# Block 1's values loaded as bands, queries in mod-3 order, and a new order of the first two blocks in a chunked-attention and gated feed-forward kernel

## The chip, the cores and the metric

The kernel runs on one core of a Trainium2 chip. The metric is the device time of one execution in microseconds, lower is better. Thirteen runs of the kernel before the change gave a median of 246.38 us (244.04 to 248.43).

## The reference

Attention in chunks of 32 queries, each seeing 16 keys to the left of its chunk, the chunk, 8 keys to the right, and 8 memory keys; then a feed-forward layer with a relu gate on the 3072 tokens of 512 features.

```python
# q, k, v: (4, 8, 768, 64); mem_k, mem_v: (4, 8, 8, 64), float32
chunk, left_ctx, right_ctx = (32, 16, 8)
for c in range(S // chunk):
    k_ctx = k[:, :, max(0, 32*c - 16):min(S, 32*c + 40)]        # v_ctx the same
    scores = 1/sqrt(D) * q_c @ concat([mem_k, k_ctx]).T
    a = softmax(scores)
    out[:, :, 32*c:32*c+32] = a @ concat([mem_v, v_ctx])
x = out.transpose(0, 2, 1, 3).reshape(3072, 512)
y = (relu(x @ w_gate) * (x @ w_val)) @ w_out                    # d_ff = 1536
```

## The kernel before

The tokens are cut into 8 blocks of 384 (half a batch element each), a block into 4 steps of 96 queries (three chunks). A step works on a band of 120 keys plus the 8 memory keys, so a score tile is 128 keys by 8 heads x 96 queries. A mask blanks the keys that a chunk may not see: either as a product on DVE after the exponent (`mask`), or as a matmul of the identity with large negative numbers ahead of the scores (L250).

For each block: `load3` loads k and q so that a partition holds three tokens in a row (768-byte runs), `cast3` casts to fp16, a turn brings features onto partitions, `bands` copies the turned keys into four bands. Queries thus come out of the turn in mod-3 order (all tokens 0, 3, 6..., then 1, 4, 7...). A step is `scores` (S), exponent `soft` (x), values (P), `norm` (n), turn of x (T) and its copy into `xT` (e). A block's feed-forward part is 12 units of `dff` (4 gate matmuls, 4 value matmuls of 384 columns, relu on ACT, product on DVE) and 3 of `outp` (12 matmuls of 512 columns).

Blocks 0 and 1 (`EARLY`) are the head. There TensorE does the turns itself. Keys of block 0 go into bands by products with a selection matrix (`keys`, L368). Values of both blocks are loaded in 768-byte runs, cast, and brought into bands by such products too (`gather_v`, L405, four steps for each block, three matmuls of 512 columns for a step; two of the eight steps take more: 28 in all), then evicted (L540). Queries are put back into natural order when they are evicted (`turn_q3` into `qp`). The memory values come by `vm16` and two transfers to the band tiles. Fillers (`keep`, tokens d2, d3, L424) are matmuls on zeros.

The schedule is manual: each engine runs its instructions in program order. In the head this order is written out in `ORDER`, one token for each piece of work (ck, cq, cv casts; key, q, kt, G products and turns; a suffix :D, :A, :P puts the copy on DVE, ACT, POOL; wa, wb, wc are loads of the feed-forward weights on POOL's queue). After `ORDER` stand 22 units for blocks 0 and 1 with hooks, of which the first ones matter here:

```python
pl(raw["k"][0:1, 0, 0, 0, 0:1], w_gate_sb[0:1, 0, 1023:1024])  # POOL, after wc's gate half has landed
load_kq(2)                                                     # waits for the line above
load_w(1024, 512)
hook = {1: cast k of block 2 on ACT, 2: the rest, turn_k(2), 3, 4: the same for q, then load_v(2, 0..3),
        4: pl(gate, w_val_sb[last column]), load_wo(0),        # POOL, after the last weights have landed
        6: bands(2, pl), 7: pl(gate, vraw...), load_wo(4), load_wo(8), ...}
su, vu = (10, 12, 14, 16), (12, 14, 16, 17)                    # units with scores and values of block 2
```

The remaining blocks run in a loop: during block n's feed-forward units, block n+1's four steps (scores at units 4, 6, 8, 10, values two units later) and block n+2's loads, casts and turns. SP's queue takes all loads but the weights, the turns by transfer, and the stores.

Of the kernel before, what the change touches and what calls it, by code (L numbers as in the profile page):

```python
# [7 lines left out]
F32 = mybir.dt.float32  # L8
# [7 lines left out]
def kernel(  # L16
# [42 lines left out]
    opool = ctx.enter_context(tc.tile_pool(name="opool", bufs=3))  # L59
# [20 lines left out]
    v16 = wpool.tile([128, 2, H, R3, D], F16, name="v16")  # L80
    kn = wpool.tile([128, 2, R3 + 1, HP, 2 * D], F16, name="kn")
    qn = wpool.tile([128, 2, HP, R3, 2 * D], F16, name="qn")
    qp = wpool.tile([128, 2, HP, MB], F16, name="qp")
    kx = wpool.tile([2 * NMEM, 2, H, D], F32, name="kx")
    vx = wpool.tile([NMEM, H, D], F32, name="vx")
    kx16 = wpool.tile([2 * NMEM, H, D], F16, name="kx16")
    vx16 = wpool.tile([NMEM, H, D], F16, name="vx16")
    vm = wpool.tile([NMEM, H, D], F32, name="vm")
    vm16 = wpool.tile([NMEM, NJ, H, VW], F16, name="vm16")
# [23 lines left out]
    neg, masks, nat = {}, {}, {}  # L113
# [18 lines left out]
    def natural_mask(name):  # L132
        nat[name] = wpool.tile([128, QB], F16, name=f"nat_{name}")
        pool.tensor_scalar(out=nat[name], in0=neg[name], scalar1=-1.0, scalar2=None, op0=ALU.is_ge)

    def product_mask(name):
        masks[name] = wpool.tile([128, QB], F16, name=f"mask_{name}")
        pool.tensor_scalar(out=masks[name].rearrange("p (t c) -> p t c", t=R3),
                           in0=neg[name].rearrange("p (c t) -> p t c", t=R3), scalar1=-1.0, scalar2=None,
                           op0=ALU.is_ge)  # L140
# [17 lines left out]
    def load_kx(eng, b):  # L158
        eng.dma_start(kx[0:NMEM, b % 2], rows(k, b, MB, NMEM))
        eng.dma_start(kx[NMEM:2 * NMEM, b % 2], mem_k[b].rearrange("h n d -> n h d"))  # L160

    def load_kq(n):
        load3(sp, "k", n)
        if n % 2 == 0:
            load_kx(sp, n // 2)
        load3(sp, "q", n)
# [31 lines left out]
    def bands(n, eng, part=range(6)):  # L198
# [25 lines left out]
        if 5 in part:  # L224
            if i == 0:
                eng(dst(3, 112, [[1, NMEM]]), src(kT, R3 * TS, [[1, NMEM]]))
            if early:
                eng(dst(0, BAND, [[128, NJ], [1, NMEM]]), src(kb_t[0], BAND, [[0, NJ], [1, NMEM]], NJ * 128))
            else:
                eng(dst(0, BAND, [[128, NJ], [1, NMEM]]), src(kT_t[0], R3 * TS + NMEM, [[0, NJ], [1, NMEM]]))  # L230
# [5 lines left out]
    class Step:  # L236
# [7 lines left out]
        def scores(self):  # L244
            i, j = self.n % 2, self.j
            if self.pm:
                m = neg[self.kd]
                m4 = bass.AP(tensor=m.tensor, offset=m.offset, ap=[m.ap[0], [0, HP], [1, QB]])
                for x in range(2):
                    pe.matmul(PS[:, self.sb + x, 0:HP * QB].rearrange("p (a c) -> p a c", a=HP), lhsT=id16, rhs=m4,  # L250
                              start=True, stop=True)
            for a in range(HP):
                for x in range(2):
                    r = slice(D * x, D * x + D)
                    o = PS[:, self.sb + x, QB * a:QB * a + QB]
                    if self.early:
                        pe.matmul(o, lhsT=self.kb[r, a, j, :], rhs=qp[r, i, a, QB * j:QB * j + QB],  # L257
                                  start=not self.pm, stop=True, skip_group_check=self.pm)
                    else:
                        pe.matmul(o.rearrange("p (t c) -> p t c", t=R3), lhsT=self.kb[r, a, j, :],  # L260
                                  rhs=qT_t[i][r, a, :, PP * j:PP * j + PP], start=True, stop=True)
# [7 lines left out]
        def mask(self):  # L269
            e = self.ex[:, :, 0:QB]  # L270
            m = (nat if self.early else masks)[self.kd]
            m8 = bass.AP(tensor=m.tensor, offset=m.offset, ap=[m.ap[0], [0, H], [1, QB]])
            dve.tensor_tensor(out=e, in0=e, in1=m8, op=ALU.mult)  # L273
# [18 lines left out]
        def turn_pe(self):  # L292
            self.t16 = PS[:, 2, 4 * VW:4 * VW + 192].bitcast(F16).rearrange("p (f c) -> p f c", f=4)
            for f in range(NFC):
                pe.transpose(self.t16[:, f], self.x[:, 128 * f:128 * f + 128], id16[0:QB, 0:QB])  # L295
# [19 lines left out]
    def product(n, m, vl_ps, g_relu):  # L315
        if n not in gvT:
            gvT[n] = gvpool.tile([128, NDC, MB], F16, name="gvT")
        if n in EARLY:
            dve.tensor_tensor(out=gvT[n][:, m], in0=vl_ps, in1=g_relu, op=ALU.mult)  # L319
        else:  # L320
            dve.tensor_tensor(out=gvT[n][:, m].rearrange("p (t j c) -> p t j c", t=R3, j=NJ),  # L321
                              in0=vl_ps.rearrange("p (j t c) -> p t j c", t=R3, j=NJ),
                              in1=g_relu.rearrange("p (j t c) -> p t j c", t=R3, j=NJ), op=ALU.mult)
# [7 lines left out]
    def outp(n, t, last=False):  # L331
        o = bank()
        for m in range(NDC):
            pe.matmul(PS[:, o], lhsT=gvT[n][:, m, 128 * t:128 * t + 128], rhs=w_out_sb[:, m, :],  # L334
                      start=(m == 0), stop=(m == NDC - 1))
        o_sb = opool.tile([128, DM], F32, name="o_sb")
        if n in EARLY:
            dst = out[n * MB + 128 * t:n * MB + 128 * t + 128, :]
        else:
            dst = bass.AP(tensor=out.tensor, offset=out[n * MB + t, 0].offset,  # L340
                          ap=[[R3 * DM, 128], [1, DM]])
# [43 lines left out]
    def turn_q3(n, a0):  # L385
# [4 lines left out]
        return qp[:, n % 2, a0:a0 + 2].rearrange("p a (i t) -> p a i t", t=R3), o.rearrange("p a t i -> p a i t")  # L390

    def cast_v3(eng, n, h0=0, nh=H):
        eng(v16[:, n % 2, h0:h0 + nh], vlong[:, n % 2, h0:h0 + nh])

    def gather_v(n, j):
        i = n % 2
        o = PS[:, bank()].rearrange("p (h d) -> p h d", h=H)
        s0 = DPAD + starts[NJ * i + j]
        mm = [(step3[:, s0 - MB * i - t:s0 - MB * i - t + BAND], v16[:, i, :, t, :]) for t in range(R3)]
        if (i, j) == (0, NJ - 1):  # L400
            mm.append((selx[0:NMEM, 0:BAND], vx16))
        if (i, j) == (1, 0):
            mm += [(step3[:, s0 - t:s0 - t + BAND], v16[:, 0, :, t, :]) for t in range(R3)]
        for e, (w, r) in enumerate(mm):
            pe.matmul(o[0:BAND], lhsT=w, rhs=r, start=(e == 0), stop=(e == len(mm) - 1))  # L405
        return vb_t[i][0:BAND, j, :, 0:D], o[0:BAND]
# [3 lines left out]
    for c in "kqv":  # L410
        load3(sp, c, 0, 0, 4)
        if c == "k":
            load_kx(sp, 0)
        if c == "q":
            sp.dma_start(vm, mem_v[0].rearrange("h n d -> n h d"))
        load3(sp, c, 0, 4, 4)
    sp.dma_start(vx, rows(v, 0, MB, NMEM))
# [10 lines left out]
    dve.memset(warm, 0.0)  # L428
    dve.memset(step3, 0.0)
    dve.memset(selx, 0.0)  # L430
    dve.memset(vm16[:, :, :, D:VW], 1.0)
    act.activation(warm, warm, ACT.Exp)
    steps(step3, -DPAD, -R3)
    steps(selx, -(BAND - NMEM), -1)
# [17 lines left out]
    for n in EARLY:  # L452
# [5 lines left out]
    load3(sp, "k", 1)  # L458
# [3 lines left out]
        kx16:A ck00:D mlast:P key0 ck01:D cq00:P key0e:A key2 key2e:A cq01:D d2 key3 vm16:D key3e:A d3 q01 q01e:A  # L462
        cv00:A d2 key1 q00 ke key1e:D q00e:A cv01:P d3 G2 vx16:P S0 kee:A ck10:P x0:A g2:D ck11:D wa:P G0 g0:A M0:D
        S1 cq10:P G1 G3 x1:A cv10:P P0 g3:A M1 cv11:P S2 g1:D kt1 cq11:D x2:A n0:D q11 d3 P1 q11e:A kt1e:D n1:D M2
        T0 q10 kt0 kt0e:D S3 e0:A q10e:A b0:D P2 T1 x3:A M3 wb:P bm:D G4 e1:A S4 n2:D P3 bi2:D T2 G5 g4:A bi0:D
        x4:A wc:P bi1:D n3:D S5 b3:P S6 g5:D e2:A T3 M4 P4 G6 x5:A S7 e3:D x6:A n4:D g6:A M5 M6:D fg01 P5 T4 n5:D
        x7:A G7 e4:A M7:D fg03 fr01:A g7:A P6 T5 fr03:A fg00 fv03 n6:D fg02 fm03:D e5:A P7 fr00:A T6 n7:D fv00 fv02
        e6:A T7 fv01 fm00:D fr02:A e7:D fg10 fm02:D fg12 fr10:A fg13 fm01:D fr12:A fg11 fr13:A fv13 fv12 fr11:A
        fv11 fm13:D fv10 fm12:D fm11:D fm10:D
    """.split()  # L470
    dve_masks = [int(t[1]) for t in ORDER if t[0] == "M" and t.endswith(":D")]
    for i, s_ in enumerate(st):
        s_.pm = i not in dve_masks
    out_of = {}
    for tok in ORDER:
# [7 lines left out]
        elif nm == "vm16":  # L483
            eng(vm16[:, :, :, 0:D], bass.AP(tensor=vm.tensor, offset=vm.offset,
                                            ap=[vm.ap[0], [0, NJ], [D, H], [1, D]]))
            sp.dma_start(vb_t[0][BAND:128], vm16)
            load3(sp, "q", 1)
            load3(sp, "v", 1)
            sp.dma_start(vb_t[1][BAND:128], vm16)
        elif nm == "vx16":  # L490
            eng(vx16, vx)
        elif nm == "mlast":
            build_mask("last", NQB - 1)
            for m in {st[i].kd: 0 for i in dve_masks}:
                natural_mask(m)
        elif nm[:2] in ("ck", "cq"):
            cast3(eng, nm[1], r[0], 2 * r[1], 2)
        elif nm[:2] == "cv":
            cast_v3(eng, r[0], 4 * r[1], 4)
# [24 lines left out]
        elif c == "w":  # L524
            if nm == "wa":
                pl(gate, raw["k"][0:1, 1, 4, 0, 0:1])
            load_w(*{"a": (0, 256), "b": (256, 256), "c": (512, 512)}[nm[1]])
# [9 lines left out]
        elif c == "G":  # L537
            out_of[nm] = gather_v(r[0] // NJ, r[0] % NJ)
# [16 lines left out]
    for m in ("first", "int", "last"):  # L555
        product_mask(m)
# [70 lines left out]
    for n in range(2, NBLK):  # L627
# [3 lines left out]
        for u in range(NDC + NT):  # L631
# [5 lines left out]
            if u >= NDC:  # L637
                for f in mid:
                    f()
                outp(n, u - NDC, last=(n == NBLK - 1 and u == NDC + NT - 1))  # L640
# [57 lines left out]
```

## Time and profile before

| | |
|---|---|
| median of 13 runs | 246.38 us |
| profiled execution | 244.04 us, span of its instructions 242.3 us |
| granted TensorE clock | 0.993 |
| TensorE busy | 231.0 us, of it L307 155.4, L334 63.5 |
| DVE, ACT, POOL busy | 111.4, 114.6, 46.8 us |
| DMA | 39.46 MB in 84414 packets, 57112 of them under 512 bytes |

Busy time is the union of an engine's instructions; matmul ends are modelled. "PEclk" is the clock that was granted to TensorE, "DMA" the mean busy share of the 16 transfer engines. An idle time is put down to the engine or transfer that ended it. SPq and POOLq are the queues on which transfers are issued.

### The profile page before, as it was taken

Reading aid. Unit: us, or ns where it says so; the run is one execution under the profiler, and the core shown is the slowest. Engines: PE = TensorE matmul, PEld = TensorE weight load, DVE = VectorE, ACT = ScalarE, POOL = GpSimd, SP = SyncE. Lnnn points to the kernel's source line nnn. Section 1 sums busy time; section 2 is a strip of 40 time slices with the busy share of each in tenths; the row PEclk is TensorE's granted clock in tenths of the full one; section 3 lists DMA queues with packets and bytes.
Section 4 is the critical chain, followed back from the end, with each engine's and each line's share of the span. In section 5 each row is a group of like instructions: output and inputs, shape, how many; then the busy total and the mean of one; then the engine's idle time right before and its main releaser. Section 6 shows DMA issues by size and latency. Waiting matters only on the chain.

```text
span 242.3 us, 4600 instructions
## 1 busy us (share of the span) xinstructions
PE 231.0 (95%) x1751; PEld 129.6 (53%) x1751; DVE 111.4 (46%) x233; ACT 114.6 (47%) x199; POOL 46.8 (19%) x102
## 2 busy tenths in 40 slices
PE   7698899999999999999999999998999999999992
PEld 5456565555554556545554555454554556456540
DVE  3347664535840067704871277404780387214300
ACT  3276663564535355445663457344644455133410
POOL 6676520126000231005000510005000500000000
PEclk9799999999999999999999999999999999999999
DMA  5999999699999998689944997199916501220012
GB/s 140 330 275 159 159 233 226 129 189 177 163 283 225 254 261 218 134 176 255 248 100 106 239 273 150 32 197 320 214 38 148 127 4 32 78 87 0 1 43 88
DMA packets 84414, 39.46 MB, mean 163 GB/s; under 512 B 57112, under 2 KB 81432, under 8 KB 84392
## 3 DMA queue, kind: packets, MB, share of 16 engines
q1 hardware_dynamic: 78440, 34.32, 58.8%
q0 software_dynamic: 5808, 4.72, 13.4%
q8 instruction: 13, 0.21, 0.4%
q10 hardware_dynamic: 144, 0.13, 0.2%
q14 instruction: 9, 0.07, 0.1%
HBM read 30.05 MB, written 6.29 MB: 150 GB/s over the span
## 4 chain that ended last, share of the span: by engine, by line
PE 88%; DMA 5%; POOL 2%; DVE 2%; ACT 1%; issue 1%; SPq 1%; ACTq 0%; DVEq 0%; POOLq 0%
PE PS L307 50%; PE PS L334 24%; PE PS L277 4%; PE PS L260 3%; DMA kT<-kn 3%; PE PS L405 2%; DMA kraw<-in_k_dram 2%; PE PS L368 1%; POOL kb L213 1%; PE PS L257 1%; DVE x_big L286 1%; PE PS L424 1%; PE PS L295 1%; PE PS L250 1%; PE PS L389 1%
## 5 line engine op out<-in xcount | busy, mean ns | idle before, releaser
L307 PE MATMUL PS<-xT,w_gate_sb 128*128 128x384 f16 x384 | 77.9, 327 | 0.0
L307 PE MATMUL PS<-xT,w_val_sb 128*128 128x384 f16 x384 | 77.5, 326 | 0.0
L321 DVE TENSOR_TENSOR gvT<-PS,g_relu 128x384 f16<-128x384 f32 x72 | 39.9, 555 | 81.0 <-PE PS L307 66.8
L312 ACT ACTIVATE g_relu<-PS 128x384 f16<-128x384 f32 x96 | 47.2, 492 | 51.6 <-PE PS L307 29.5
L334 PE MATMUL PS<-w_out_sb,gvT 128*128 128x512 f16 x288 | 63.5, 379 | 0.0
L307 PEld LDWEIGHTS <-w_gate_sb 128*128 128x128 f16 x384 | 35.5, 98 | 24.3 <-DVE xT L298 0.3
L307 PEld LDWEIGHTS <-w_val_sb 128*128 128x128 f16 x384 | 36.3, 98 | 22.5 <-issue 0.2
L334 PEld LDWEIGHTS <-gvT 128*128 128x128 f16 x288 | 27.7, 98 | 32.3
L213 POOL COPY kb<-kT 128x480 f16<-128x480 f16 (+1 forms) x18 | 13.7, 859 | 109.5 <-DMA kT<-kn 109.5
L348 ACT COPY o_sb<-PS 128x512 f32<-128x512 f32 x23 | 13.5, 586 | 44.9 <-PE PS L334 40.7
L266 ACT ACTIVATE ex<-PS 128x768 f16<-128x768 f32 x32 | 25.9, 812 | 9.0 <-PE PS L260 7.9
L286 DVE TENSOR_TENSOR x_big<-PS,rinv 96x512 f16<-96x512 f32 x32 | 22.0, 686 | 1.1
L319 DVE TENSOR_TENSOR gvT<-PS,g_relu 128x384 f16<-128x384 f32 x24 | 13.2, 554 | 12.2 <-PE PS L307 12.0
L277 PEld LDWEIGHTS <-ex 128*128 128x128 f16 x256 | 11.7, 98 | 5.9 <-ACT g_relu L312 2.2
L277 PE MATMUL PS<-vb,ex 128*128 128x66 f16 x256 | 13.4, 194 | 0.6 <-ACT xT L298 0.2
L283 DVE RECIPROCAL rinv<-PS 96x8 f32<-96x8 f32 x32 | 6.4, 201 | 11.7 <-PE PS L277 9.0
L177 ACT CAST kn<-kraw 128x768 f16<-128x768 f32 x12 | 9.9, 825 | 0.6 <-DMA kraw<-in_k_dram 0.6
L177 ACT CAST qn<-qraw 128x768 f16<-128x768 f32 x12 | 10.0, 833 | 0.0
L273 DVE TENSOR_TENSOR ex<-ex,mask_int 128x768 f16<-128x768 f16 x18 | 9.8, 545 | 0.0
L260 PEld LDWEIGHTS <-kb 64*128 64x128 f16 x192 | 4.8, 94 | 8.5 <-issue 7.0
L260 PE MATMUL PS<-qT,kb 64*128 64x96 f16 x192 | 8.3, 205 | 0.8 <-POOL kb L230 0.8
L184 DVE CAST vb<-vraw 128x1024 f16<-128x1024 f32 x12 | 8.3, 689 | 0.0
(103 smaller groups left out, 116.2 us busy)
## 6 DMA issues: line engine op xcount, KB each, us to landing
out_dram<-o_sb SPq DMA_DIRECT2D x23, 256.0 KB
vraw<-in_v_dram SPq DMA_DIRECT2D x24, 240.0 KB
kraw<-in_k_dram SPq DMA_DIRECT2D x7, 768.0 KB
qraw<-in_q_dram SPq DMA_DIRECT2D x7, 768.0 KB
w_out_sb<-in_moe_w_out_dram POOLq DMA_DIRECT2D x3, 512.0 KB, 5.9
w_gate_sb<-in_moe_w_gate_dram POOLq DMA_DIRECT2D x2, 512.0 KB, 8.3
w_val_sb<-in_moe_w_val_dram POOLq DMA_DIRECT2D x2, 512.0 KB, 11.4
kraw<-in_k_dram SPq DMA_DIRECT2D x2, 384.0 KB
```

Of the source, the lines that this page charges most:

```text
L177: eng(d.rearrange("p a t (x d) -> p a x t d", x=2), raw[c][:, i, 2 * a0:2 * a0 + 2 * na].rearrange("p (a x) t d -> p a x t d", x=2))
L213: eng(dst(1, r, [[128, nj], [R3, 40]]), src(kT, TS * t + P + (r > 0), [[PP, nj], [1, 40]]))
L260: pe.matmul(o.rearrange("p (t c) -> p t c", t=R3), lhsT=self.kb[r, a, j, :], rhs=qT_t[i][r, a, :, PP * j:PP * j + PP], start=True, stop=True)
L266: act.activation(self.ex[:, :, 0:QB].rearrange("p (h b) c -> p b h c", b=2), PS[:, self.sb:self.sb + 2, 0:HP * QB].rearrange("p b (h c) -> ...
L277: pe.matmul(PS[:, 2 + h // 4, VW * (h % 4):VW * (h % 4) + VW], lhsT=self.ex[:, h, :], rhs=self.vb[:, self.j, h, :], start=True, stop=True)
L286: dve.tensor_tensor(out=self.x.rearrange("p (b h d) -> p b h d", b=2, h=4), in0=o[:, :, :, 0:D], in1=rb, op=ALU.mult)
L307: pe.matmul(o, lhsT=w_sb[:, f, 128 * m:128 * m + 128], rhs=xTs[n][:, f], start=(f == 0), stop=(f == NFC - 1))
L312: act.activation(g_relu, g_ps, ACT.Relu)
L319: dve.tensor_tensor(out=gvT[n][:, m], in0=vl_ps, in1=g_relu, op=ALU.mult)
L321: dve.tensor_tensor(out=gvT[n][:, m].rearrange("p (t j c) -> p t j c", t=R3, j=NJ), in0=vl_ps.rearrange("p (j t c) -> p t j c", t=R3, j=NJ ...
L334: pe.matmul(PS[:, o], lhsT=gvT[n][:, m, 128 * t:128 * t + 128], rhs=w_out_sb[:, m, :], start=(m == 0), stop=(m == NDC - 1))
L348: act.copy(o_sb, PS[:, o])
```

## The change

- Block 1's values are loaded straight as four bands of 120 rows (256-byte runs) and cast; block 0's still go by `gather_v`, which now also brings in the memory values (a matmul of 16 or 8 rows in each step). The memory rows of block 1's band tile come by one transfer from `vx` in on-chip memory (`lvm`).
- Queries of the head stay in mod-3 order (`qT`), as do masks, products and stores; the branches for `EARLY` fall away.
- x is turned into the rotating banks instead of a corner of bank 2.
- The four loads of 8 rows (`kx`, `vx`) are issued on ACT's queue; `ORDER` and the order of loads on SP are new; the first weights are loaded in two pieces of 128 columns.
- Six output buffers instead of three; in the loop, values that fall into an output product are issued after its fourth matmul.

```diff
-    opool = ctx.enter_context(tc.tile_pool(name="opool", bufs=3))
+    opool = ctx.enter_context(tc.tile_pool(name="opool", bufs=6))
...
-    def load_kx(eng, b):
-        eng.dma_start(kx[0:NMEM, b % 2], rows(k, b, MB, NMEM))
-        eng.dma_start(kx[NMEM:2 * NMEM, b % 2], mem_k[b].rearrange("h n d -> n h d"))
+    def kx_rows(eng, b, d, t, mem):
+        eng.dma_start(d[0:NMEM], mem[b].rearrange("h n d -> n h d"))
+        eng.dma_start(d[NMEM:2 * NMEM], rows(t, b, MB, NMEM))
...
-                    if self.early:
-                        pe.matmul(o, lhsT=self.kb[r, a, j, :], rhs=qp[r, i, a, QB * j:QB * j + QB],
-                                  start=not self.pm, stop=True, skip_group_check=self.pm)
-                    else:
-                        pe.matmul(o.rearrange("p (t c) -> p t c", t=R3), lhsT=self.kb[r, a, j, :],
-                                  rhs=qT_t[i][r, a, :, PP * j:PP * j + PP], start=True, stop=True)
+                    pe.matmul(o.rearrange("p (t c) -> p t c", t=R3), lhsT=self.kb[r, a, j, :],
+                              rhs=qT_t[i][r, a, :, PP * j:PP * j + PP], start=not self.pm, stop=True,
+                              skip_group_check=self.pm)
...
-            self.t16 = PS[:, 2, 4 * VW:4 * VW + 192].bitcast(F16).rearrange("p (f c) -> p f c", f=4)
+            self.t16 = PS[:, bank(), 0:192].bitcast(F16).rearrange("p (f c) -> p f c", f=4)
...
-    def outp(n, t, last=False):
+    def outp(n, t, last=False, mid=()):
         o = bank()
         for m in range(NDC):
+            if m == 4:
+                for f in mid:
+                    f()
...
-        return qp[:, n % 2, a0:a0 + 2].rearrange("p a (i t) -> p a i t", t=R3), o.rearrange("p a t i -> p a i t")
+        return qT_t[n % 2][:, a0:a0 + 2], o
...
+    def gather_v(j):
         o = PS[:, bank()].rearrange("p (h d) -> p h d", h=H)
+        s0 = DPAD + starts[j]
+        x = slice(0, 2 * NMEM if j == NJ - 1 else NMEM)
+        mm = [(selx[x], vx16[x], o)]
+        mm += [(step3[:, s0 - t:s0 - t + BAND], v16[:, :, t, :], o[0:BAND]) for t in range(R3)]
...
-    for c in "kqv":
-        load3(sp, c, 0, 0, 4)
-        if c == "k":
-            load_kx(sp, 0)
-        if c == "q":
-            sp.dma_start(vm, mem_v[0].rearrange("h n d -> n h d"))
-        load3(sp, c, 0, 4, 4)
-    sp.dma_start(vx, rows(v, 0, MB, NMEM))
+    dve.memset(warm, 0.0)
+    act.activation(warm, warm, ACT.Exp)
+    kx_rows(act, 0, kx[:, 0], k, mem_k)
+    kx_rows(act, 0, vx, v, mem_v)
+    LOADS = "lq01 lk00 lk01 lq00 lk1 lv01 lv00 lq1 lvm lv11 lv10 lv12 lv13".split()
+    for tok in LOADS:
+        c, r = tok[1], [int(ch) for ch in tok if ch.isdigit()]
+        if tok == "lvm":
+            sp.dma_start(vraw[BAND:128, 1].rearrange("p j h d -> p j (h d)"),
+                         bass.AP(tensor=vx.tensor, offset=vx.offset, ap=[[vx.ap[0][0], NMEM], [0, NJ], [1, H * D]]))
+        elif len(r) == 1:
+            load3(sp, c, r[0])
+        elif c == "v" and r[0] == 1:
+            sp.dma_start(vraw[0:BAND, 1, r[1]], rows(v, 0, starts[NJ + r[1]], BAND))
+        else:
+            load3(sp, c, r[0], 4 * r[1], 4)
...
+        cq01:A kx16:A q01 ck00:D q01e:D vx16:P ck01:D key1 cq00:A key1e:D key0 ck11:D key0e:A key3 ck10:P key3e:A
+        d3 key2 q00 ke key2e:A q00e:D d3 kt1 S0 kt0 cv01:A kee:D mlast:P kt1e:A cv00:D S1 kt0e:D x0:A d3 G0 b0:D G1
+        x1:A g0:A M0:D S2 cq11:D g1:A P0 x2:A cq10:D M1 G2 q11 n0:D bi1:P S3 wa:P bi2:D bi0:D wA:P g2:A P1 x3:A q10
+        q11e:D M2 q10e:A G3 g3:A wb:P n1:D bm:D P2 T0 M3:D S4 T1 cv10:A n2:D e0:D wc:P d2 P3 x4:A e1:D S5 n3:D T2
+        S6 M4 x5:A M5 T3 b3:D e2:D cv11:P e3:A P4 S7 n4:D x6:A cv12:P fg00 P5 cv13:P fr00:A x7:A M6 fv00 n5:D
+        fm00:D fg01 P6 fr01:A n6:D T5 T4 e5:A fv01 M7 P7 fm01:D T6 n7:D e4:A fg03 e6:A fr03:A fv03 fm03:D T7 fg02
+        fv02 e7:A fr02:A fg13 fm02:D fr13:A fg12 fv13 fm13:D fr12:A fg11 fv12 fg10 fv11 fr11:A fr10:A fm12:D fv10
+        fm11:D fm10:D
...
             if nm == "wa":
-                pl(gate, raw["k"][0:1, 1, 4, 0, 0:1])
-            load_w(*{"a": (0, 256), "b": (256, 256), "c": (512, 512)}[nm[1]])
+                pl(gate, GATE)        # GATE = raw["q"][0:1, 1, 0, 0, 0:1]
+            if nm == "wa":
+                load_w(0, 128)
+            elif nm == "wA":
+                load_w(128, 128)
+            else:
+                load_w(*{"b": (256, 256), "c": (512, 512)}[nm[1]])
```

## The prediction

> **What bounds the kernel now.** I read the page's engine rows and slices first, then the chain in order of time, TensorE's waits, and last a table by stage.
>
> ```profile
> span 242.3 us, 4600 instructions
> PE 231.0 (95%) x1751; PEld 129.6 (53%) x1751; DVE 111.4 (46%) x233; ACT 114.6 (47%) x199; POOL 46.8 (19%) x102
> ...
> PE   7698899999999999999999999998999999999992
> ...
> PEclk9799999999999999999999999999999999999999
> DMA  5999999699999998689944997199916501220012
> ```
>
> TensorE is busy for 95% of the span. Its gaps lie in the first six slices of 6.06 us and near 167 us. The DMA row is as full in slices 2 to 15: up to about 90 us two resources are nearly full, after that TensorE alone.
>
> The chain (start, us, what):
>
> ```profile
> 2.11 5.37 DMA kraw<-in_k_dram
> 7.50 0.57 DVE kn L177
> ...
> 8.12 1.52 PE PS L368 x8
> ...
> 12.42 0.75 PE PS L368 x8
> ...
> 37.97 19.00 PE PS L307 x116
> 56.97 0.30 PE PS L260 x8
> ```
>
> The head waits for the second half of k, issued as the fourth transfer, until 7.50. One key product (L368) then takes 1.52 us, and 0.75 later. From 38 us the chain is matmuls without a hole. The last row is the first score of block 2.
>
> TensorE's own waits, and three answers of the timeline (weights' queue; POOL before block 2's scores):
>
> ```profile
> PE PS L368 <- DVE kn L177: 2.2, 1, 2.2
> ...
> PE PS L295 <- DVE x_big L286: 1.0, 1, 1.0
> PE PS L260 <- POOL kb L230: 0.8, 1, 0.8
> PE PS L257 <- POOL kb L223: 0.7, 1, 0.7
> ...
> 22.01 0.75 POOL L447 DMA_DIRECT2D w_gate_sb<-in_moe_w_gate_dram  x1
> ...
> 44.66 0.75 POOL L450 DMA_DIRECT2D w_out_sb<-in_moe_w_out_dram  x1
> ...
> 56.57 0.30 POOL L230 COPY kb<-kT 128x128 f16<-128x128 f16 x1
> ```
>
> The waits are small singles, 5.2 us in all with 0.3 and 0.2 at L295 and L277. The last row matters most: block 2's key bands end at 56.87 and its first score starts at 56.93. That pair has no slack.
>
> By stage (us, PE, PEld, DVE, ACT, POOL busy, granted clock, DMA share, GB/s):
>
> ```profile
> 5.00:10.00 5.00, 2.81 (x20) 1.60 (x20) 0.56 (x1) 1.30 (x3) 4.57 (x16) 0.77 1.07 332
> 10.00:15.00 5.00, 5.00 (x52) 3.34 (x50) 2.38 (x3) 3.46 (x6) 1.55 (x3) 0.89 0.90 245
> ...
> 44.00:47.00 3.00, 3.00 (x20) 1.83 (x19) 1.44 (x3) 1.53 (x3) 0.93 (x2) 1.00 0.24 42
> 50.00:54.00 4.00, 4.00 (x26) 2.43 (x25) 1.67 (x3) 2.29 (x5) 0.71 (x1) 1.00 1.12 205
> ```
>
> The full DMA row means 332 GB/s with 768-byte runs, and 205 with the 256-byte runs of block 2's values.
>
> **Part 1, TensorE's work in the head.** The first real product starts at 5.00. Unit 0 of the dense loop starts ten units (80 matmuls of 19.00/116 = 0.164 us) before 56.97, at 43.9. Of those 38.9 us, 4.4 are waits (2.2, 1.0, 0.7, 0.3, 0.2), and about 1.6 is the slow clock: 1.52 and 1.29 instead of 0.75 for two key products, the rest for fillers. That leaves 32.9 us of work.
> - Gathers (L405): 28 matmuls become 16, since block 1's four bands no longer pass through TensorE. Three took 0.65 us, so 12 x 0.217 = -2.6 us. The evictions of block 1 (four, of 0.6 to 0.7 us) become four casts of the loaded bands of 0.6 us, one on ACT and three on POOL. No net change there.
> - Masks by TensorE: five steps become six, two more matmuls, +0.3. Fillers: 33 to 31, -0.2. Transposes, key products and scores keep their numbers.
> - New work: 30.4 us.
>
> **Part 2, when it starts and what it waits for.** The first half-load landed at 4.2 (DVE's first cast starts then). After the change that load is half of q; ACT then issues its fourth small load (0.43), which waits for it, and casts (0.83): the first transposes start near 5.5. Later half-loads follow at 1.2 us each (0.39 MB at 332 GB/s): k at 5.4 and 6.7 to 7.3 instead of 7.5, q complete near 8.5 instead of 10.06, block 1's k near 10.5 instead of 14.8. Walking the order: 0.2 us for the first k cast, 0.6 for the second, about 0.7 until values and their casts, 1.5 for exponent-to-values and x chains of the kind that cost 2.3 now: 3.0 us of idle. No gap is as long as the present one, so no slow clock is charged. Unit 0 at 5.5 + 30.4 + 3.0 = 38.9, against 43.9: -5.0 us (bounds: -6.5 with half the idle, -2 with twice as much).
>
> The Trainium skill (TensorE: Matmul & The Clock Gate, "Why this matters for your kernels") asks for no idle gap above about 3 us. The trace lost its clock after a gap of 2.2, so I use the trace: 1.6 us come back in my sum; by the rule the slow stage had nothing to do with that gap and could stay, and the gain would be 3.4.
>
> **Part 3, the DMA stream.** Block 1's values were 0.79 MB in 768-byte runs (2.4 us at 332 GB/s) and become 4 x 120 x 8 runs of 256 bytes, 0.98 MB: 4.8 us at 205 GB/s, so +2.4. The skill (DMA: Bandwidth & Descriptors, "Why small descriptors are slow") puts 27% on a 256-byte descriptor: 4.1 us, +1.7. The trace is taken. This speaks against the change: it lies ahead of, and beside, the weights. Against it, the weights' second pair now waits at 22.01 behind POOL's casts of block 1's values; afterwards these casts stand behind the weight issues, and the first four narrow issues and the next pairs follow from about 15.5 on, after q of block 1 lands (17.7 now). The pair at 22.01 goes out near 19. It took 9.4 us from there to the landing that releases block 2's loads (31.46); with some 0.5 us of value bands still moving, that lands near 29: the stream moves up by 2.5 us only.
>
> TensorE thus gains 5.0, the stream 2.5. Where do they meet? The first w_out issue (44.66) waits on the last weights, not on TensorE, so it moves to about 42. Block 2's key turn (issued at 48.53, landed 53.3) follows ACT's casts in the dense loop, so it moves to 43.5. Today they are 3.9 us apart and hardly overlap; then 1.5, and for about 2.5 us they share the engines at half rate each, so the turn lands 1.3 to 2.5 us late. Queued behind it are POOL's bands (3.6 us), and behind those, with no slack, block 2's scores: TensorE idles +1.7. Query casts of block 2 may wait up to 0.5 us on ACT ahead of the relus; the PSUM banks cover that, uncovered it costs the same 0.5. Later blocks follow the loop's own pace; those bands end 1.2 us before their scores (86.8 against 88.1), so up to 1 us more could go there. I charge none.
>
> **Part 4, the rest.** SP loses the kx, vm, vx and two vb transfers (0.43, 0.27, 0.41, 1.77, 0.76, 1.57 us of queue), ACT gets four issues of 0.4 to 0.5 while it has nothing else until 4.2; uncovered, they delay the first cast, which I charged. SP gets lvm and four bands; it waits for vx first, with only the bands behind it, and they are due near 20. Moved masks on POOL (0.44 each) are hidden: POOL is idle between 9.98 and 12.54 now. Values in the middle of an output product: five boundaries with 0.09 us of issue in the chain, -0.4; x of that step comes 0.9 us later, under about 3 us of cover before the next block reads it. Six output buffers: two waits of ACT, 4.2 us, near 81 us; TensorE had no wait there, so 0 (bounds -0.5, 0). The turned-query layout and strided products: same shapes, 554 against 555 ns, 0. The x turns in rotating banks: the single x wait is worth -1.0 at most, a bank wait +0.5; inside the idle above. The wait at 167 us (0.8) stays.
>
> Sum: -5.0 + 1.7 - 0.4 = -3.7. The profiled execution (span 242.3, 244.04 with what lies around it) gives 240.3. The median, 246.38, stands 2.3 above that run; the change off it gives 242.7.
>
> **The rivals.** A change under 0.5% (1.2 us) can't be told here.
> - Main case: the head gains about 5, block 2 gives part back. 242.7, chance 0.50.
> - All of the head's gain stays (the turn lands in time): -5.4, 241.0. For it: DMA idles between 44 and 47 now (share 0.24). Chance 0.15.
> - The DMA stream binds through block 3: TensorE's gain shrinks to the stream's 2.5 less 1.2 at the next bands: -1.3, 245.1; with the last weights no earlier, 0. For it: DMA rows of 9 to slice 15. Chance 0.20, half of it within 0.5%.
> - Slower: the small k loads on ACT's queue. SP has issued five loads of 2.36 MB by then. If the small ones are served after those, they land near 2 + 7.1 = 9.1, or 11.1 with the 2.0 us by which k's second half took longer from issue (5.37) than the first (3.4); before, issued second and third, they were there at 4.77. ACT holds their cast (0.62) ahead of q's second half and of all key evictions, so the first key product ends near 11.8, not 6.7: +5.1, and a gap that long costs a slow stage, +1.6. With -5.0 and -0.4 that is +1.3: 247.7. It decides from a landing past about 10. The skill (Trainium Kernel Development and Optimization, "Key Constraints") has the queues interleave on the same engines, which speaks against it; no trace here shows the two mixed. Chance 0.15.
>
> Faster: 0.50 + 0.15 + half of 0.20, less 0.03 for the main case's edge: 0.72. Same: 0.10. Slower: 0.15 and that 0.03: 0.18. The range runs from the second case with 1.5 us for the unknown idle, 239.5, to short of the last, 247.2.
>
> **What would show it.** Right: gathers 16, first transposes at 5.4 to 5.7, clock 1.00 from 5 to 15 us, unit 0 near 39, first block-2 score (L252) near 53 to 54.5 with a wait on POOL's kb of 1 to 2.5 us. Wrong: kx cast later than 7 us; a wait on vb or weights over 1.5 us in the head; a stage at half clock; block-3 scores waiting over 1 us; unit 0 after 41.

## The result and the profile after

The changed kernel takes 244.2 us (median of 11 runs, 241.22 to 247.28). Against the runs of the kernel before beside it (246.75) the ratio is 0.9887, 95% interval 0.9853 to 0.9921: faster by 1.1%, some 2.8 us, where 3.7 were forecast. In a second group of runs the ratio was 0.9899 (0.9862 to 0.9935). Medians here are over all runs of a kernel; ratios and their intervals leave disturbed runs out.

The profiled execution of the kernel after (244.03 us) lies near its median. That of the kernel before (244.04) was the fastest of its thirteen. So the two traces have one span, 242.3 us, and differ only in where the time lies.

From the page of the kernel after:

```profile
span 242.3 us, 4579 instructions
PE 229.9 (95%) x1739; PEld 128.8 (53%) x1739; DVE 112.1 (46%) x231; ACT 114.2 (47%) x197; POOL 47.7 (20%) x104
...
PE   6899899985999999999999999999999999999992
...
PEclk9799999998899999999999999999999999999999
DMA  6999999799999999749971996689945501220012
```

The head's early holes are smaller. A new hole, the digits 8 and 5 of the PE row, stands in the ninth and tenth slice, and the clock drops right behind it. TensorE's waits and the chain (start, us, what) name it:

```profile
PE PS L252 <- POOL kb L226: 4.0, 1, 4.0
PE PS L378 <- ACT qn L173: 1.3, 1, 1.3
PE PS L419 <- DVE zero L421: 1.3, 1, 1.3
PE PS L300 <- ACT ex L259: 0.9, 1, 0.9
PE PS L357 <- DVE kn L173: 0.4, 1, 0.4
```

```profile
44.06 0.83 ACT kn L173
44.95 8.69 DMA kT<-kn
53.76 2.68 POOL kb L209 x3
57.72 4.22 PE PS L300 x16
...
72.01 12.95 PE PS L327 x60
84.96 5.20 PE PS L300 x32
...
110.87 5.20 PE PS L300 x32
...
136.79 5.20 PE PS L300 x32
```

Before, no transfer stood in the chain at this place, and the same later points came earlier:

```profile
69.93 12.95 PE PS L334 x60
82.88 5.20 PE PS L307 x32
...
109.05 5.20 PE PS L307 x32
```

Now the turn of block 2's keys stands in the chain, with 8.69 us, and POOL's bands behind it. The timeline has the turn, w_out's first load and the bands, first before, then after:

```profile
48.53 2.45 SPq L191 DMA_TRANSPOSE kT<-kn  x1
...
53.29 2.69 POOL L213 COPY kb<-kT 128x480 f16<-128x480 f16 x3 [7.88 <-DMA kT<-kn]
```

```profile
44.95 2.30 SPq L187 DMA_TRANSPOSE kT<-kn  x1
45.04 0.76 POOL L444 DMA_DIRECT2D w_out_sb<-in_moe_w_out_dram  x1
...
53.76 2.68 POOL L209 COPY kb<-kT 128x480 f16<-128x480 f16 x3 [7.96 <-DMA kT<-kn]
```

From the issue of the turn to the first band it was 4.8 us before, with w_out's load 3.9 us ahead of the turn (44.66), and it is 8.8 now. The kernel after stage by stage (PE, PEld, DVE, ACT, POOL busy, granted clock, DMA share, GB/s):

```profile
5.00:10.00 5.00, 3.31 (x23) 1.85 (x24) 2.30 (x4) 2.34 (x4) 2.46 (x9) 0.75 1.10 321
10.00:15.00 5.00, 5.00 (x62) 3.40 (x60) 2.15 (x5) 3.33 (x6) 3.51 (x10) 0.91 1.10 318
44.00:47.00 3.00, 3.00 (x20) 1.82 (x19) 1.12 (x3) 2.75 (x6) 0.93 (x2) 1.00 0.47 99
50.00:54.00 4.00, 3.39 (x21) 1.83 (x19) 1.77 (x4) 1.47 (x3) 0.24 (x1) 1.00 1.26 196
```

Both traces against one another, in us:

| place | before | after | difference |
|---|---|---|---|
| unit 0 of the dense loop | 43.8 | 40.2 | -3.6 |
| first score of block 2 | 56.93 | 57.38 | +0.45 |
| long run of output products | 69.93 | 72.01 | +2.08 |
| first 32 dense matmuls of the loop | 82.88 | 84.96 | +2.08 |
| period of a loop block (five of them) | 26.16 | 25.92 | -1.25 in all |
| wait at 167 us | 0.77 | none | -0.8 |

In these two traces the head gains 3.6. Block 2's first score takes it all back and 0.45 more, and the half-clock stage behind that wait takes another 1.6 to 1.7. The loop returns 2.05, so the sum is nothing. One trace of a kernel is not its usual execution, though: in the six traces that have the head of the kernel after unchanged, unit 0 stood between 40.2 and 41.9. No run separates what in the head brought how much (the gathers, the queries' layout, the new order).

### The profile page after: what moved, and what is told of

It is laid out like the page before. It is cut to its first block, busy times and chain, and to the rows that moved or that the text cites. A ratio compares the mean times of both kernels' runs of the same rounds, so it can differ in the third digit from the quotient of the medians.

```text
span 242.3 us, 4579 instructions
## 1 busy us (share of the span) xinstructions
PE 229.9 (95%) x1739; PEld 128.8 (53%) x1739; DVE 112.1 (46%) x231; ACT 114.2 (47%) x197; POOL 47.7 (20%) x104
## 4 chain that ended last, share of the span: by engine, by line
PE 89%; DMA 6%; POOL 1%; ACT 1%; DVE 0%; issue 0%; SPq 0%; POOLq 0%
PE PS L300 49%; PE PS L327 26%; PE PS L252 4%; DMA kT<-kn 4%; PE PS L270 3%; DMA kraw<-in_k_dram 2%; PE PS L357 2%; PE PS L391 2%; POOL kb L209 1%; PE PS L246 1%; PE PS L288 1%; PE PS L419 1%; PE PS L378 0%; ACT kn L173 0%; PE PS L371 0%
## 5 line engine op out<-in xcount | busy, mean ns | idle before, releaser
L300 PE MATMUL PS<-xT,w_val_sb 128*128 128x384 f16 x384 | 78.8, 329 | 0.9 <-ACT ex L259 0.9
L300 PE MATMUL PS<-xT,w_gate_sb 128*128 128x384 f16 x384 | 78.8, 329 | 0.0
L327 PE MATMUL PS<-w_out_sb,gvT 128*128 128x512 f16 x288 | 64.3, 379 | 0.0
L209 POOL COPY kb<-kT 128x320 f16<-128x320 f16 (+1 forms) x20 | 15.5, 862 | 108.3 <-DMA kT<-kn 108.0
L252 PE MATMUL PS<-qT,kb 64*128 64x96 f16 x256 | 11.1, 207 | 4.0 <-POOL kb L226 4.0
L173 ACT CAST qn<-qraw 128x768 f16<-128x768 f32 x14 | 11.7, 833 | 5.5 <-DMA qraw<-in_q_dram 5.5
L252 PEld LDWEIGHTS <-kb 64*128 64x128 f16 x256 | 6.5, 95 | 14.1 <-issue 8.9
L270 PE MATMUL PS<-vb,ex 128*128 128x66 f16 x256 | 13.4, 194 | 0.0
L266 DVE TENSOR_TENSOR ex<-ex,mask_int 128x768 f16<-128x768 f16 x19 | 10.4, 545 | 0.0
L419 PE MATMUL PS<-zero 128*128 128x248 f16 x31 | 5.5, 333 | 1.3 <-DVE zero L421 1.3
```

The costliest lines, as they stand in the source:

```text
L173: eng(d.rearrange("p a t (x d) -> p a x t d", x=2), raw[c][:, i, 2 * a0:2 * a0 + 2 * na].rearrange("p (a x) t d -> p a x t d", x=2))
L209: eng(dst(1, r, [[128, nj], [R3, 40]]), src(kT, TS * t + P + (r > 0), [[PP, nj], [1, 40]]))
L270: pe.matmul(PS[:, 2 + h // 4, VW * (h % 4):VW * (h % 4) + VW], lhsT=self.ex[:, h, :], rhs=self.vb[:, self.j, h, :], start=True, stop=True)
L300: pe.matmul(o, lhsT=w_sb[:, f, 128 * m:128 * m + 128], rhs=xTs[n][:, f], start=(f == 0), stop=(f == NFC - 1))
```

## Experiments

**Where the head's gain goes: w_out's load moved behind block 2's bands.**

```diff
 4: [..., lambda: load_v(2, 3),
-         lambda: pl(gate, w_val_sb[0:1, 0, DFF - 1:DFF]), lambda: load_wo(0)],
+         ],
-6: [lambda: bands(2, pl)],
+6: [lambda: bands(2, pl), lambda: pl(gate, w_val_sb[0:1, 0, DFF - 1:DFF]), lambda: load_wo(0)],
```

> The changed kernel with one edit: the first w_out load is issued behind POOL's bands of block 2 instead of at the landing of the last weights (45.0 us), so that it no longer shares the engines with the turn of block 2's keys. Theory (collision): the turn lands after about 4.8 us as it did before, not 8.7; the wait of 4.0 us ahead of block 2's first score goes to under 1, and 2 to 4 us are gained against the changed kernel (ratio to before 0.975 to 0.98), unless w_out then comes late for the first output products, near 66 us: that gives back 0 to 2 us. Rival (the turn is slow by itself, or the query turn is what holds it): the turn still takes over 8 us and the time stays at 0.989 or grows.

Measured: 241.76 us, ratio 0.9794 (0.9744 to 0.9844), clear of the kernel after. The trace is of the slowest of its six runs (245.53), with unit 0 at 41.9. The turn went out at 47.70 and the bands began at 52.2: 4.5 us from issue instead of 8.8.

```profile
47.70 2.03 SPq L187 DMA_TRANSPOSE kT<-kn  x1
...
52.16 2.69 POOL L209 COPY kb<-kT 128x480 f16<-128x480 f16 x3 [4.49 <-DMA kT<-kn]
```

TensorE no longer waited for the bands. That w_out's load beside it slows the turn is shown: over all 14 traces, the eight in which that load left between 0.7 us ahead of the turn and 1.7 behind it have 7.3 to 8.8 us from the turn to the bands, the six in which it left 3.4 us or more ahead, or behind the bands, 4.5 to 4.8. In this trace some time went again further on: DVE's cast of block 2's values waited 2.75 us for its load, and TensorE behind it.

**The values of block 2 loaded ahead of its key turn**, on top of that edit.

```diff
     load_kq(2)
+    for j in range(NJ):
+        load_v(2, j)
...
 4: [lambda: cast3(ac, "q", 2, 2, 2), lambda: turn_q(2),
-    lambda: load_v(2, 0), lambda: load_v(2, 1), lambda: load_v(2, 2), lambda: load_v(2, 3)],
+    ],
```

> The kernel with w_out's first load behind block 2's bands (as in the run before), and block 2's values loaded on SP's queue right behind block 2's k and q, ahead of its key turn, in place of behind its query turn. Theory 'that kernel lost again at the values': the wait of DVE's cast of block 2's values (2.75) and TensorE's waits behind it (1.3, 0.7, 0.5) and the half-clock stage near 69 to 72 are gone; first block-2 score at 55.8 to 56.5, median 240 to 241.2. Rival 'the values only change places with the turn': the four value loads (eight transfers, about 8 us of SP's issuing, 1.2 MB) hold SP or the engines when the key turn is due, it lands at 53.5 or later, the first block-2 score waits to 57.5 or later, and the median is 242 to 244.

244.51 us, 0.9869 (0.981 to 0.9927): the rival. The turn left only at 48.44, behind the value loads, and TensorE waited 3.0 us for the bands. The same kernel with 27 fillers instead of 20:

> Both edits together: w_out's first load behind block 2's bands, block 2's values ahead of its key turn, and 27 fillers in place of 20 ahead of the first transposes. If the head's 1.5 us from the clock and the repaired block 2 add up, the median is 1 to 1.5 us under that of the same kernel without the fillers (239 to 240). If block 2's keys then bind (its turn can't start earlier because the loads of its k and q follow the weights, not TensorE), the head's gain is waited away at block 2's first score and the two medians are within 0.5 us.

243.26 us, 0.9819 (0.9756 to 0.9881). The intervals of the two overlap, so nothing is decided on their difference.

**What paces the weight stream: block 1's values in one long load.** One load of 768-byte runs in place of the four bands; the value tiles of block 1 then hold other rows than the reference asks for. The transfer of the memory rows and the casts are fitted to that buffer (left out here).

```diff
-LOADS = "... lv00 lq1 lvm lv11 lv10 lv12 lv13"
+LOADS = "... lv00 lq1 lv1 lvm"
...
```

> The changed kernel, with block 1's values moved by one load of 768-byte runs (0.79 MB) in place of the four loads of 256-byte runs (0.98 MB). The casts read the same buffer, so block 1 gets other rows as its values: that part of the computation is wrong, the work of every engine is the same. Theory (the 256-byte runs hold up the weight stream): the bands took 2.4 us more of the engines by the trace of before, so the landing that releases block 2's loads comes 2 to 3 us sooner than 32.15 and the wait at block 2's first score falls from 4.0 to 1.5 to 2.5, ratio to before 0.98. Rival (the stream is set by POOL's late first issue, which waits for q of block 1): it moves by under 1 us and the wait stays near 4.

242.3 us, 0.9828 (0.9768 to 0.9888). The landing that releases block 2's loads came at 31.67 against 32.15: 0.5 us, and no 2 to 3. In the seven traces whose weight stream is that of the kernel after, this landing lies anywhere between 30.7 and 33.2, so the 0.5 can't be told from nothing. TensorE still waited 2.9 us before block 2's first score, here for the turn of the queries. The time lies below that of the kernel after, but the intervals overlap.

**The first weights gated on block 1's k again.** In the kernel before this gate was k, and the first weights left at 15.73. The change gated them on q, whose transfer stands behind three value and key loads: 17.70. (`bi0` is on POOL in the kernel after, as in the line below; the diff in the section on the change has DVE there.)

```diff
-GATE = raw["q"][0:1, 1, 0, 0, 0:1]
+GATE = raw["k"][0:1, 1, 4, 0, 0:1]
...
-... ck10:P key3e:A ... S3 wa:P bi2:D bi0:P wA:P g2:A
+... ck10:P wa:P wA:P key3e:A ... S3 bi2:D bi0:P g2:A
```

> The kernel after, with the first four weight transfers gated on block 1's k (landed near 11.7) in place of block 1's q (landed near 17.2), and issued right behind POOL's cast of that k, near 13.4 instead of 17.7 and 20.1. Theory 'POOL's first issue sets the weight stream': the transfer that releases block 2's loads (32.15) lands near 28 to 29, the last weights near 41 to 42 instead of 44.8, block 2's key turn meets w_out's first load no more or less, and the median is 1 to 2 us shorter. Rival 'the transfers are short of engine time': the DMA share is full from 5 to 32 us already, so weights issued earlier only take the time of the value bands and of block 1's q; the release stays at 31.3 to 32.2, block 1's scores or values wait for their loads by 0.5 to 2 us, and the median is 244 to 246.

241.97 us, 0.9779 (0.9729 to 0.983), clear of the kernel after in both of its groups. The weights left at 13.05. Yet the release came at 31.51, inside the spread of the traces without this edit (30.7 to 33.2), and POOL waited 2.1 us for block 1's values: the trace bears out the rival (the engines are short of time), the time bears out the theory. Unit 0 stood at 39.3, the turn left at 43.99 instead of 44.95. This profiled execution was the slowest of the six, with a wait of 3.7 us and two half-clock stages at block 2, so it doesn't show where the typical gain lies.

**The clock: fillers up to the first transposes.**

```diff
-keep(20)
+keep(27)
```

> The kernel after, with 27 fillers in place of 20 ahead of the first transposes: at 0.18 us each they end at about 6.2 instead of 4.94 and close the 1.30 us gap in which TensorE waits for the first cast of q. Theory 'the gap lowers the clock': the half-clock stage from 7.5 to 10.9 us is gone, the first three key products take 0.75 to 0.80 us each instead of 1.09, 1.38 and 1.33, unit 0 of the dense loop starts at about 38.6 instead of 40.2. What becomes of it at block 2 is open: block 2's key turn is then issued 1.5 us earlier, still behind the weights, so its first score moves from 57.4 to somewhere between 56 and 57.4; median 242.7 to 244.2. Rival 'the stage has another cause' (the ramp of the load, a fixed time after the start): the products stay at 1.1 to 1.4 us, unit 0 stays at 40.2, the median at 244.2.

243.09 us, 0.9843 (0.9792 to 0.9893). Key products took 0.78 to 0.79 us, as the theory has it. But they also did in the traces of two kernels without these fillers (the re-gated one and the one with early values). And unit 0 stood at 40.7, no earlier, with waits of 0.6, 0.7 and 0.6 elsewhere. The gain isn't shown. So the kernel after was run again:

> The kernel after once more, on the same chip as the two before it, to compare medians and to see whether the half-clock stage from 7.5 to 10.9 us belongs to it. If a gap near 1.3 us ahead of the first transposes always lowers the clock, the first three key products take 1.1 to 1.4 us again; if the stage comes and goes, they take near 0.79. The wait before block 2's first score should be 3 to 4.5 us in either case. Median 244.2 within 1 us.

244.47 us. No slow stage at 7.5 to 10.9, but one at 10.0 to 13.4, behind a wait of 1.73. What decides this is told in the last section.

**Values inside the output product.** This part alone on the kernel before, then the kernel after without it:

```diff
-                for f in mid:
-                    f()
-                outp(n, u - NDC, last=(n == NBLK - 1 and u == NDC + NT - 1))
+                outp(n, u - NDC, n == NBLK - 1 and u == NDC + NT - 1, mid)
```

> The kernel before, with one part of the change alone: in the loop, values that fall into an output product are issued after its fourth matmul. From the trace after, five block periods shrank from 26.16 to 25.91 us, so theory A (this part stands alone): 1.25 us faster than before, ratio near 0.995. Rival B, my record: the five boundaries are worth 0.09 us each, 0.4 us, nothing that can be told. Rival C: x of that step is 0.9 us later and the next block's first unit waits for it: slower by up to 1 us.

> The changed kernel with that one part undone (values ahead of the output product again). Theory A: 1.25 us slower than the changed kernel, so about 0.994 of before if the changed kernel is at 0.989, with a wait of about 0.25 us before the values at five block ends. If the median gain came from this part alone and the head gave nothing (rival D), this kernel ties with before.

Alone: 244.6 us, 0.992 (0.9881 to 0.9959). Without it: 245.25 us, 0.992 (0.988 to 0.996). The loop's period decides it: 25.92 us with the part on either kernel, 26.17 without it on either. That is 0.25 for each of five blocks, 1.25 us. The interval of the first run holds this sum. The weight-load row of TensorE in the kernel after without this part shows what it hides:

```profile
103.85 0.32 PEld L270 LDWEIGHTS <-ex 128*128 128x128 f16 x8 [0.45 <-ACT g_relu L305]
```

The values need the masked exponents of their step, and DVE finishes that mask only just before (in the kernel before it ran from 100.17 to 100.71, the weight load at 100.83). Four output matmuls put ahead of them cover the wait.

**A better order for block 2's keys.** Their loads are released by an earlier weight column, and both casts come one unit earlier.

```diff
-pl(raw["k"][0:1, 0, 0, 0, 0:1], w_gate_sb[0:1, 0, 1023:1024])
+pl(raw["k"][0:1, 0, 0, 0, 0:1], w_gate_sb[0:1, 0, 511:512])
...
-0: [lambda: cast_kx(pl, 1)],
-1: [lambda: cast3(ac, "k", 2, 0, 2)],
-2: [lambda: cast3(ac, "k", 2, 2, 2), lambda: turn_k(2)],
+0: [lambda: cast_kx(pl, 1), lambda: cast3(ac, "k", 2, 0, 2)],
+1: [lambda: cast3(ac, "k", 2, 2, 2), lambda: turn_k(2)],
```

> The kernel after, with two edits for block 2's keys: its loads of k and q wait for weight columns up to 511 in place of 1023 (they stand at 32.35 now and would go out near 27), and the two casts of k come one dense unit earlier, so that the turn follows unit 1 instead of unit 2 (issue near 43.5 instead of 44.95, ahead of w_out's first load). Theory 'block 2's keys take the head's gain': the turn lands at 48.5 to 50.5 instead of 53.64, the first block-2 score starts at 53.3 to 54.5 (unit 0 plus 13.1) with a wait under 1 us, the half-clock stage behind the wait is gone, median 240 to 242. Rival 'the engines are short of time': the weights for unit 0 and the last weights are pushed back by the 1.6 MB put ahead of them (5 to 7 us), TensorE waits for weights at unit 0 by 1 to 3 us, the turn shares with the last weights and lands at 52 or later, median 243.5 to 246.

242.42 us, ratio 0.9754 (0.9682 to 0.9826), which rests on three of the six runs. The trace is of one of the other three (244.28). TensorE's wait for the bands fell to 1.5, and no slow stage followed. The turn, issued at 44.66 with w_out's load at 45.05, still took 7.6 us; part of the shorter wait comes from unit 0, which stood at 41.2 there. A wait of 1.5 for w_out came later. With the first weights gated on k too:

> The kernel with block 2's k and q loaded earlier and turned behind unit 1, with the first four weight transfers gated on block 1's k as well. If the two edits act at different places (unit 0 near 39.3 instead of 40.2 by the one, no wait at block 2's first score by the other), the medians add: 0.5 to 1.5 us under the kernel with block 2's keys alone, near 239 to 240.5. If the gate on k only helped by moving block 2's loads up, the two kernels are within 0.5 us.

239.65 us (239.12 to 240.9), 0.9717 (0.9661 to 0.9772): better than both kernels, and the lowest median of all. Against the kernel without the gate on k the ratio moved by 0.4% and the intervals overlap, so that the two edits add up is not shown. Its page, and the stage of block 2's first score:

```profile
PEclk9999999999999999999999999999999999999999
```

```profile
49.87:53.28 3.41, 2.80 (x18) 1.47 (x15) 1.62 (x3) 1.06 (x3) 2.11 (x3) 1.00 1.06 210
53.28:56.70 3.42, 1.90 (x18) 1.19 (x19) 0.10 (x2) 1.24 (x2) 1.68 (x6) 1.00 1.27 168
56.70:60.11 3.41, 3.41 (x35) 2.03 (x33) 2.95 (x7) 1.73 (x3) 1.89 (x2) 1.00 1.19 157
```

The clock stays full throughout; a wait of 2.1 remains, since the turn, issued at 43.60, again meets w_out's load (42.87). Last, that load moved behind the bands here too:

> The kernel with block 2's keys early and the first weights gated on block 1's k, with w_out's first load moved behind block 2's bands as well. There the key turn went out at 43.60, 0.7 us after w_out's first load, and took 7.5 us; TensorE still waited 2.1 us for the bands. Theory 'the shared engines still cost': alone the turn takes 4.5 to 5, lands near 48.5, and the wait of 2.1 is gone; median 237.5 to 238.7. Rival 'w_out has no slack left': its three loads (3.1 MB with 1.2 MB of values ahead, 18 to 20 us from 52) land near 70 or later, the first output products of block 0 or 1 wait for them by 1.5 to 3 us, and the median is 239.3 to 241.

240.32 us, 0.9728 (0.9673 to 0.9784): no different. Turn and bands, by POOL and SP rows of the timeline:

```profile
44.17 2.05 SPq L187 DMA_TRANSPOSE kT<-kn  x1
...
48.63 2.68 POOL L209 COPY kb<-kT 128x480 f16<-128x480 f16 x3 [5.74 <-DMA kT<-kn]
...
52.28 0.75 POOL L444 DMA_DIRECT2D w_out_sb<-in_moe_w_out_dram  x1
```

The turn took 4.5 us and the wait of 2.1 was gone. In its place came 1.7 us of others between 62 and 68 us (0.9 for `gvT`, 0.7 for `ex`, 0.2 for w_out): DVE's second cast of block 2's values waited 2.3 us for its load. The loads behind the turn have no slack either. (The page lists 512 KB for each w_out load, half of what this expectation put down.)

## Why the prediction was right, and where its steps were off

The direction held, and so did both ends of the mechanism: the head gains, and block 2 gives back, because its key turn meets w_out's load and POOL's bands stand behind it without slack. But the forecast was that block 2 gives back a third of the head's gain; in the trace it gives back all of it. That the medians still moved by 2.8 us, near the 3.7 forecast, is in part luck: a gain in the head reckoned too high and a collision reckoned too low stand against a gain in the loop that was reckoned at a third. Of the signs of being right that the prediction named, only the 16 gathers came; the first transposes, unit 0, the clock and block 2's first score all missed their figures, and one of the signs of being wrong, a stage at half clock, came twice. Six terms were off.

- **Start, 5.5.** The first half of q landed near 5.0, not 4.2, and the first transposes started at 6.25:

```profile
5.04 0.28 ACTq L156 DMA_DIRECT2D vx<-in_v_dram  x1
5.37 0.83 ACT L173 CAST qn<-qraw 128x768 f16<-128x768 f32 x1 [3.06 <-DMA qraw<-in_q_dram]
6.17 0.62 ACT L478 CAST kx<-kx 16x512 f16<-16x512 f32 x1
...
6.25 0.51 PE L378 MATMUL PS<-id,qn 128*128 128x128 f16 x6 [1.30 <-ACT qn L173]
7.19 1.09 PE L357 MATMUL PS<-step,kn 128*128 128x360 f16 x6 [0.43 <-DVE kn L173]
```

- **Work 30.4, idle 3.0, slow clock 0.** From 6.25 to 40.2 the trace has 1.4 us of idle and one half-clock stage (3.4 us long, so 1.7 lost); the work is the rest, 30.9. The "-1.6 of clock" did not come: both traces have one half-clock stage in the head. The idle was half as long, and so unit 0 came at 40.2 instead of 38.9. By the skill's rule the gain would have been 3.4 and it was 3.6; but that is not for the rule's reason, as the last section shows.
- **The stream, "moves up by 2.5".** It did not move up: release 32.15 against 31.46 before, with 30.7 to 33.2 in the other traces of this stream. The step that failed is the time at which q of block 1 lands: 17.2, not 15.5. The first weights thus left 2.0 us later than before (17.70 against 15.73), and this price of the new gate was not charged; put back on k and issued right behind its cast, the kernel is 1.1% faster by the two ratios. The "205 with the 256-byte runs of block 2's values" was read from a window in which the first value load left only at 52.72; most of it is the two turns. From 56 to 59, when the last value load leaves (56.58), it is 198, so the figure itself stands.
- **Collision, +1.7.** It was 4.0. The last weights landed at 44.80 instead of 42, so w_out's load left 0.1 us after the turn, not 1.5 ahead of it, and the turn took 8.69 us where 6 to 7.3 were reckoned. A cost that stood nowhere in the sum came behind it: the half-clock stage, 1.7.
- **Values inside the output product, -0.4.** It was -1.25. The 0.09 of issue in the chain was the wrong row; the wait stood in the weight load, 0.45 in front of L277, which the chain doesn't carry.
- **The wait at 167 us, "stays".** It went, -0.8. Neither the kernel before with the output products' part alone nor the kernel after without it has that wait, so it can belong to the one execution of the kernel before that was traced; why is open.

Costed at nothing: the strided product (555 ns) shows no change, rightly, and block 3's bands put no wait in front of its scores. For the six output buffers the trace of before shows no wait of TensorE either. The other trace with three buffers, the slowest run of the kernel before with the output products' part alone (246.93), does, behind a store:

```profile
86.02 2.83 DMA out_dram<-o_sb
```

```profile
PE PS L307 <- ACT o_sb L351: 0.8, 1, 0.8
```

What they are worth in a usual execution is not shown.

The slower rival, k's small loads late on ACT's queue, was wrong: they were issued at 0.97 and 1.57, and their cast followed q's at 6.17 without a wait. The rival in which the DMA stream binds was half right. Block 2's first score moved by less than 0.5 us while unit 0 moved by 3.6; the transfers paid out none of TensorE's gain there. Its forecast of 245.1 was nearer to the measured 244.2 than the main case's 242.7; by the change against the runs beside it (2.8 us), the main case's 3.7 is nearer than its 1.3.

One thing stays open: why the two profiled executions have one span while the medians are about 2.5 us apart. There is one trace of the kernel before, its fastest run; what its usual execution loses beyond that is not in it. In the one other trace with the old head (246.93, see above) unit 0 stood at 45.3 instead of 43.8, behind a half-clock stage from 21.8 to 25.2; one execution decides nothing.

## What to carry to other kernels

When a head is shortened, look first at the earliest transfer chain that the next block needs (load, cast, turn, bands) and ask what sets its start: here two gates on loads and the place of two casts brought another 1.7% by the ratios, more than the 1.1% of the whole change. A gate moved in passing is a change of its own and needs its own line in the sum. And a wait in front of the matrix engine can cost more than its length, if the clock falls behind it.

## What the runs showed of the hardware

**The granted clock is set in stages of 3.41 us, and less idle than expected lowers it.** In all traces the stages follow one another in a fixed raster, whose place differs from execution to execution (the first stage at full clock began between 4.1 and 10.6 us). The Trainium skill (TensorE: Matmul & The Clock Gate, "What's actually happening") has such a window, 3.4 us long and running free of the kernel, and asks for at least one idle window before the clock falls. The length agrees; the idle that is needed does not. Kernel after (two places), its second run, the run with early values and fillers, and the one with w_out late, cut along their rasters (columns as above):

```profile
4.12:7.53 3.41, 1.67 (x17) 1.09 (x15) 0.99 (x2) 1.43 (x2) 3.07 (x13) 1.00 1.10 330
7.53:10.95 3.42, 3.42 (x21) 1.75 (x18) 1.32 (x3) 1.42 (x2) 0.39 (x2) 0.50 1.10 321
...
55.32:58.73 3.41, 1.35 (x15) 0.89 (x16) 0.00 (x0) 0.97 (x2) 2.00 (x5) 1.00 1.32 158
58.73:62.15 3.42, 3.42 (x19) 1.50 (x17) 2.02 (x4) 0.76 (x2) 1.67 (x3) 0.50 1.13 127
```

```profile
6.60:10.01 3.41, 1.73 (x16) 1.08 (x17) 1.63 (x3) 0.00 (x0) 1.11 (x4) 1.00 1.09 321
10.01:13.43 3.42, 3.37 (x18) 1.81 (x17) 0.56 (x1) 1.90 (x3) 1.46 (x2) 0.50 1.10 327
```

```profile
51.15:54.56 3.41, 1.53 (x10) 0.69 (x8) 1.12 (x2) 0.60 (x2) 2.67 (x4) 1.00 0.62 118
54.56:57.97 3.41, 2.47 (x22) 1.56 (x23) 0.61 (x2) 1.27 (x3) 3.30 (x8) 1.00 0.23 20
```

```profile
65.21:68.62 3.41, 1.41 (x20) 0.72 (x19) 3.18 (x7) 1.30 (x2) 0.00 (x0) 1.00 1.31 174
68.63:72.04 3.41, 3.41 (x14) 1.20 (x11) 1.52 (x4) 0.00 (x0) 0.00 (x0) 0.50 1.12 316
```

Idle is the first number less PE's. At 1.74 and 2.06 idle the next stage has half the clock; at 1.68 too, where TensorE was kept waiting once for 1.73. In the third fence 1.88 did not lower it, in the last one 2.00 did, gathered from several short waits. Over all traces the stages with under 1.6 us of idle at full clock were followed by full clock, those with 2.0 or more by half, and between 1.6 and 2.0 both occurred (1.68 to 1.80 lowered it, 1.88 and 1.93 did not). A stage already at half, with 1.55 idle, was followed by another at half. One stage at half costs 1.7 us (half of 3.41). So half a window of idle is about enough, and it is the sum within a stage that counts, not the longest gap; the rule that the prediction weighed (no gap above about 3 us) lets through what these traces show to be enough. And one and the same wait of 2.8 us passed unpunished where the raster cut it in two (third fence), while in the run without the fillers 2.7 of a wait of 3.0 lay within one stage, and half the clock followed. Part of the spread between executions of one kernel may come from this; no run here isolates it.

**A turn by transfer took 7.3 to 8.8 us, from its issue to the first instruction behind it, beside a load of w_out on POOL's queue, and 4.5 to 4.8 without one near it** (eight traces and six). From 50 to 54 us the kernel after had a DMA share of 1.26 at 196 GB/s.
